# The second half of the last output block is stored through ScalarE's DMA queue

## The chip, the cores and the metric

One core of one Trainium2 chip runs the kernel. Its engines are TensorE (PE, with its weight loads PEld), VectorE (DVE), ScalarE (ACT), GpSimd (POOL) and SyncE (SP); SP computes nothing and issues DMAs. The metric is the time of one execution on the device in microseconds (us), as the median of several runs. A profile shows one execution more closely: its span runs from the first to the last instruction of the program.

## What is computed

Sparse attention over 4 batches of 8 heads, 768 positions and 64 channels a head, followed by a gated linear layer. All tensors are fp32. The reference, cut down:

```python
scores = scale * np.matmul(q, k.transpose(0, 1, 3, 2)) - slopes * dist
scores = np.where(is_global | is_local, scores, -1e9)      # 8 global, 96 local keys
a = softmax(scores)
x = np.matmul(a, v)                                        # then (4, 768, 512)
gate = sigmoid(causal depthwise conv of x with 5 taps)
out = (gate * (x @ w_val)) @ w_out                         # (4, 768, 512)
```

## The kernel before

The sequence of each batch is cut into two halves of three blocks of 128 rows, so there are eight phases (`phases`, `ph` 0 to 7). For each phase the kernel computes the attention of four pairs of heads, the convolution, the gate, the value product (`val`, L930) and the output product (`outp`, L957), which leaves each block of 128 rows by 512 columns in PSUM. ACT or DVE copies it to SBUF (`evac_o`, L969) and SP stores it to HBM (`store`, L981). All instructions stand in one straight line; the order of all of them is written out in the table `ORDER`, and each engine executes its own in that order.

The last phase is treated apart. Its three blocks are named `LATE` and live in the tiles `late[0]` to `late[2]`. The last of them is cut into two halves of 256 columns (`parts` gives 2 for this block alone and 1 for every other), with `h` 0 and 1: two smaller groups of matmuls, two smaller copies on ACT and two smaller stores. So `h` is 1 for one store of the program.

The stores of the late blocks do not stand in the straight line. Before them stands a branch, `tc.If(slow[0])` at L1114: a flag, read from a tile on every engine, says whether inputs lie outside what the fast path covers. If it is set, the function `general` computes everything again. Otherwise all engines jump over `general`. After the branch SP issues the four late stores, in the order block 0, block 1, block 2 with h 0, block 2 with h 1 (`for key in behind_general: store(*key)`, L1118). A hint to load the code behind the branch early is given to SP, ACT and DVE (L1110).

On each engine the jump is followed by a short piece of code that brings the semaphores to the counts that the other path would have left: SP does this for the eight semaphores `DMAHW0` to `DMAHW7`, which the landings of DMAs raise in turn, and ACT for its own counter of finished instructions. At the very end (line L1345, where the program is closed) SP waits for the eight DMA semaphores by number, one instruction each, and then all five engines meet in a barrier. In the kernel before, no engine but SP issues a DMA.

Of the kernel before, what the change touches and what calls it, by code (L numbers as in the profile page):

```python
# [132 lines left out]
P = 128  # L133
# [144 lines left out]
def attention_moe(ctx, tc, qT, kT, kg, vw, v, counts_in, wt, wb, out):  # L278
    nc = tc.nc
# [81 lines left out]
    T = {}  # L361
# [17 lines left out]
    def width(s):  # L379
        return P if block(*steps[s]) == 0 else WIN  # L380
# [42 lines left out]
    for ph in range(NPH):  # L423
        todo = [(g, k) for g in range(ph * NP, ph * NP + NP) for k in range(blocks(g))]
        n = BATCH[phases[ph][2]]
# [101 lines left out]
    def biases(e, h, part):  # L527

        cols = slice(0, P) if part == 0 else slice(P, P + WIN)
        x = -8.0 * 2.0 ** -(h + 1)  # L530
        if e == ACT:
            nc.scalar.mul(bias[:, h, cols], dist[:, cols], x)
            return
        engine(e).tensor_scalar(
            out=bias[:, h, cols], in0=dist[:, cols], scalar1=x, scalar2=1.0, op0=ALU.mult, op1=ALU.mult,
        )

    for h in range(H):
        for part, cost in enumerate(({DVE: 0.13, POOL: 0.34, ACT: 0.24}, {DVE: 0.19, POOL: 0.42, ACT: 0.28})):
            plan.add(("BIAS", h, part), 3 * (h // 2) + part - 1 + 0.1 * (h % 2), cost,  # L540
                     lambda e, h=h, part=part: biases(e, h, part), [("DIST", part)])
# [180 lines left out]
    def chunks(q, k):  # L722
        n = pieces(step[2 * q, k])[0]
        return [(j, c) for j in range(2) for c in range(n)]
# [72 lines left out]
    for q in range(NPAIR):  # L797
        for k in range(blocks(2 * q)):
# [4 lines left out]
            n = len(chunks(q, k))  # L803
# [5 lines left out]
    for g, (ph, p) in enumerate(groups):  # L809
        for k in range(blocks(g)):  # L810
            s = step[g, k]
            n = width(s)
# [141 lines left out]
    def parts(ph, k):  # L954
        return 2 if (ph, k) == (NPH - 1, phases[ph][2] - 1) else 1
# [25 lines left out]
    def store(ph, k, h):  # L981
        b, k0, _ = phases[ph]
        r0, n = (k0 + k) * P, DM // parts(ph, k)
        if (ph, k) in LATE and not general_is_behind:
            behind_general.append((ph, k, h))
            return
        w = n // (2 if ph in IN_TWO else 1)
        for c in range(0, n, w):
            nc.sync.dma_start(out[b, r0 : r0 + P, h * n + c : h * n + c + w], T["ob", ph, k, h][:, c : c + w])

    sent = []

# [29 lines left out]
    def add_outputs(ph):  # L1022
# [6 lines left out]
        for k in range(nk):  # L1029
            for h in range(parts(ph, k)):  # L1030
                n = parts(ph, k)
                for c in range(NC):
                    key = ("OM", ph, k, h, c)
                    deps = [("GH", ph, c), ("GL", ph, c), ("WP", NC + c), ("WH", NC + c)]
                    if c:
                        bank = [("OM", ph, k, h, c - 1)]
                    elif (ph, k) == (NPH - 1, nk - 1):
                        bank = [("FC",)]
                    else:
                        bank = plan.ring("moe", 2, key, [("OE", ph, k, h)])  # L1040
                    deps += bank
                    if ph == 0 and c == 0:
                        deps += [("WP", NC + i) for i in range(NC)]
                    if (ph, k, h, c) == (NPH - 1, 0, 0, 0):
                        deps += [("FV",)]
                    plan.add(key, u + U_O + O_T * (4 * k + c) / 12 + 0.5 * h, {PE: 0.649 / n},
                             lambda e, ph=ph, k=k, h=h, c=c: outp(ph, k, h, c), deps)
                    if c == 0:
                        plan.opening(key, bank)
                key = ("OE", ph, k, h)  # L1050
                plan.add(key, u + U_O + U_OE * (k + 1), {ACT: 0.6 - 0.215 * h} if (ph, k) in LATE else {ACT: 0.6 - 0.215 * h, DVE: 0.605 - 0.25 * h},
                         lambda e, ph=ph, k=k, h=h: evac_o(e, ph, k, h),
                         [("OM", ph, k, h, NC - 1)] + ([] if (ph, k) in LATE else plan.ring("ob", 3, key, [("ST", ph, k, h)])))
                key = ("ST", ph, k, h)
                plan.add(key, u + U_O + U_OE * (k + 1), {SP: 0.5}, lambda e, ph=ph, k=k, h=h: store(ph, k, h),
                         [("OE", ph, k, h)] + ([("BR",)] if (ph, k) in LATE else []), P * DM * 4 // n)
                if (ph, k) not in LATE:
                    sent.append(key)
# [59 lines left out]
    for key in behind_general:  # L1118
        store(*key)
# [229 lines left out]
```

## Time and profile before

| | |
|---|---|
| median of 3 runs | 251.1 us (250.1 to 251.37) |
| the profiled execution | 249.76 us |
| its span | 248.0 us |
| PE, DVE, ACT, POOL busy | 96%, 86%, 72%, 53% of the span |
| q1, the DMA queue that SP feeds | 23040 packets, 45.21 MB |

The profiled execution lies 1.3 us under the median of the runs, and 1.76 us of it lie outside its span. An engine's name with a q, as ACTq or SPq, stands for its sequencer: waits on semaphores, branches, and the issue of DMAs. Such instructions are not counted as busy time. A DMA has a start (its issue), a duration (how long the sequencer took to issue it) and a time to landing (from the issue to the last of the 16 DMA engines reporting).

### The profile page before, as it was taken

The page shows a single profiled execution, that of the slowest core. Times are in us where ns is not written, and L with a number is a line of the kernel's source. Part 1 is how long each engine was busy: PE and PEld are TensorE (multiplying, and loading weights), DVE is VectorE, ACT ScalarE, POOL GpSimd, SP SyncE. Part 2 cuts the span into 40 slices and gives each one's busy share as a digit, 9 for nine tenths or more (in the row PEclk, how much of TensorE's full clock was granted, in tenths as well). Part 3 has the DMA queues.
Part 4 walks back from the last instruction along what each step waited for, and adds up shares of the span by engine and source line. Part 5 has one row for each costly group of instructions (what it writes and reads, how often), then busy time and mean ns, then how long its engine had stood idle before and what let it go on. Part 6 is the DMA issues. An engine that isn't in the chain of part 4 may idle for free.

```text
span 248.0 us, 10366 instructions
## 1 busy us (share of the span) xinstructions
PE 238.8 (96%) x4037; PEld 204.7 (83%) x4041; DVE 213.4 (86%) x822; ACT 179.6 (72%) x600; POOL 130.4 (53%) x264
## 2 busy tenths in 40 slices
PE   8998788999999999999999999999999999999993
PEld 3556577888899888988899788898899889988993
DVE  3997999998979989898989989898979979989620
ACT  3999899998998488877967589886678388422202
POOL 6989999999317530364064533455419741810220
PEclk9999999999999999999999999999999999999999
DMA  5999598161298054529558289791079507200303
GB/s 181 401 397 386 200 336 284 36 187 52 61 306 306 3 186 186 167 100 272 187 172 256 84 272 345 221 312 48 7 261 402 200 25 227 73 4 0 127 8 134
DMA packets 23095, 45.94 MB, mean 185 GB/s; under 512 B 2688, under 2 KB 13696, under 8 KB 23040
## 3 DMA queue, kind: packets, MB, share of 16 engines
q1 hardware_dynamic: 23040, 45.21, 53.4%
q8 instruction: 34, 0.56, 0.9%
q14 instruction: 21, 0.17, 0.2%
HBM read 38.91 MB, written 6.29 MB: 182 GB/s over the span
## 4 chain that ended last, share of the span: by engine, by line
PE 80%; DVE 12%; POOL 4%; DMA 1%; issue 1%; ACT 0%; SPq 0%; DVEq 0%; POOLq 0%
PE o L963 26%; PE val L935 25%; PE x L765 11%; PE s L685 9%; PE pt L734 5%; PE pt L737 4%; DVE gate L881 3%; DVE t L693 3%; POOL p L720 3%; DVE wh L562 2%; DMA counts_i<-in_counts 1%; DVE xl L872 1%; DVE wy L557 1%; POOL wvh L328 1%; DVE wy L565 1%
## 5 line engine op out<-in xcount | busy, mean ns | idle before, releaser
L720 POOL TENSOR_SCALAR p<-p,rs 128x168 f32<-128x168 f32 (+1 forms) x152 | 66.3, 450 | 55.1 <-DVE rs L714 36.4
L704 ACT ACTIVATE p<-t,mins 128x168 f32<-128x168 f32 (+1 forms) x192 | 81.5, 430 | 13.8 <-DVE mins L693 12.2
L881 DVE SCALAR_TENSOR_TENSOR gate<-x,cwt,gate 128x384 f32<-128x384 f32 x128 | 76.2, 614 | 1.1
L693 DVE CUSTOM_DVE_ANT_0 t<-s,bias 128x168 f32<-128x168 f32 (+1 forms) x192 | 54.1, 318 | 7.6 <-PE s L685 7.5
L935 PE MATMUL val<-xh,wvh 128*128 128x384 f32 x128 | 44.4, 347 | 0.2 <-DVE gate L944 0.2
L326 ACT COPY a<-pt 128x384 f32<-128x384 f32 (+2 forms) x79 | 35.3, 473 | 11.7 <-PE pt L734 7.6
L935 PE MATMUL val<-xl,wvh 128*128 128x384 f32 x128 | 41.8, 327 | 0.0
L935 PE MATMUL val<-xh,wvl 128*128 128x384 f32 x128 | 41.7, 326 | 0.0
L963 PE MATMUL o<-woh,gh 128*128 128x512 f32 (+1 forms) x100 | 39.1, 391 | 0.0
L704 ACT ACTIVATION_READ_ACCUMULATOR p<-t,mins 128x1 f32 x192 | 37.6, 196 | 0.0
L963 PE MATMUL o<-woh,gl 128*128 128x512 f32 (+1 forms) x100 | 37.2, 372 | 0.0
L963 PE MATMUL o<-wol,gh 128*128 128x512 f32 (+1 forms) x100 | 37.1, 371 | 0.0
L765 PEld LDWEIGHTS x<-a,v 56*64 56x64 f32 (+1 forms) x2112 | 33.7, 135 | 4.0 <-issue 1.1
L685 PE MATMUL s<-rk,rq 64*64 64x168 f32 (+1 forms) x768 | 35.8, 304 | 1.1 <-issue 0.9
L765 PE MATMUL x<-a,v 56*64 56x64 f32 (+1 forms) x2112 | 35.8, 219 | 0.8 <-DVE x L863 0.7
L685 PEld LDWEIGHTS s<-rk,rq 64*64 64x64 f32 x768 | 25.8, 132 | 8.9 <-issue 6.0
L952 POOL TENSOR_TENSOR gl<-gate,gh 128x384 fp32r<-128x384 f32 x24 | 24.1, 1008 | 11.8 <-ACT gh L326 5.0
L935 PEld LDWEIGHTS val<-xh,wvh 128*128 128x128 f32 x128 | 24.2, 189 | 1.8 <-DVE gate L944 0.5
L935 PEld LDWEIGHTS val<-xl,wvh 128*128 128x128 f32 x128 | 24.2, 189 | 0.5 <-DVE xl L872 0.2
L935 PEld LDWEIGHTS val<-xh,wvl 128*128 128x128 f32 x128 | 24.2, 189 | 0.0
L944 DVE SCALAR_TENSOR_TENSOR gate<-gate,val 128x384 f32<-128x384 f32 x32 | 17.4, 549 | 4.7 <-PE val L935 4.5
L963 PEld LDWEIGHTS o<-wol,gh 128*128 128x128 f32 x100 | 18.9, 189 | 2.4
(101 smaller groups left out, 351.0 us busy)
## 6 DMA issues: line engine op xcount, KB each, us to landing
v<-in_vw SPq DMA_DIRECT2D x40, 384.0 KB, 5.6
rq<-in_qT SPq DMA_DIRECT2D x32, 192.0 KB, 5.3
rk<-in_kT SPq DMA_DIRECT2D x16, 252.0 KB, 4.8
out<-ob SPq DMA_DIRECT2D x15, 256.0 KB, 4.8
w<-in_wb SPq DMA_DIRECT2D x7, 512.0 KB, 5.8
again<-in_wb SPq DMA_DIRECT2D x7, 512.0 KB, 5.9
rk<-in_kT SPq DMA_DIRECT2D x16, 200.0 KB, 4.9
out<-ob SPq DMA_DIRECT2D x12, 128.0 KB, 1.8
```

What stands on the lines that cost most here:

```text
L326: nc.scalar.copy(dst, src)
L685: nc.tensor.matmul(T["s", step[g, k], j][half], T["rq", g][r, k * P + i * HQ : k * P + (i + 1) * HQ], T["rk", g][r, c0 : c0 + n], start=Tr ...
L693: nc.vector.tensor_tensor_reduce(out=t[:, :n], in0=T["s", s, j], in1=bias[:, h, :P] if n == P else bias[:, h, P:], op0=ALU.add, op1=ALU.mi ...
L704: nc.scalar.activation(p_of(s, j), T["t", s, j][:, :n].rearrange("p (c w) -> p c w", c=pieces(s)[0]), AF.Exp, bias=mins[:, s, j : j + 1], ...
L720: engine(e).tensor_scalar(out=pr, in0=pr, scalar1=rs, scalar2=1.0, op0=ALU.mult, op1=ALU.mult)
L734: nc.tensor.transpose(pt[n // 4][:, n % 4 * P : n % 4 * P + P], src, ident)
L765: nc.tensor.matmul(T["x", 2 * q + r][j * D : (j + 1) * D, c0 : c0 + HQ], v[rows, slot], a[rows, i, n * j + c], start=c == 0, stop=c == use ...
L881: nc.vector.scalar_tensor_tensor(out=gt, in0=src, scalar=w, in1=gt, op0=ALU.mult, op1=ALU.add)
L935: nc.tensor.matmul(T["val", ph, m], (wvh, wvh, wvl)[r][:, c, m * P : (m + 1) * P], woven((T["xh", g], T["xl", g], T["xh", g])[r][:, : size ...
L944: nc.vector.scalar_tensor_tensor(out=t, in0=t, scalar=1.0, in1=T["val", ph, m].rearrange("p (b a) -> p a b", a=2), op0=ALU.add, op1=ALU.mult)
L952: engine(e).tensor_sub(tile_of(("gl", ph, m), [P, HT], F32R, "gl", G_B)[:, :n], T["g", ph, m], T["gh", ph, m][:, :n])
L963: nc.tensor.matmul(T["o", ph, k, h], (T["gh", ph, c], T["gl", ph, c], T["gh", ph, c])[r][:, cols], woven((woh, woh, wol)[r][:, c])[:, h * ...
```

## The change

The function `store` takes its queue by `h`: SP's where `h` is 0, ACT's where it is 1. Only the last half block has `h` 1. The line numbers behind this place grow by one.

```diff
         for c in range(0, n, w):
-            nc.sync.dma_start(out[b, r0 : r0 + P, h * n + c : h * n + c + w], T["ob", ph, k, h][:, c : c + w])
+            queue = nc.scalar if h else nc.sync
+            queue.dma_start(out[b, r0 : r0 + P, h * n + c : h * n + c + w], T["ob", ph, k, h][:, c : c + w])
```

On SP, behind the branch, the stores of the late blocks stand so in the kernel before (`late_86` to `late_88` are the three late tiles; in brackets the semaphores waited for):

```order
L1114 UNCONDITIONAL_BRANCH [waits DMAHW0_49,DMAHW1_49,DMAHW2_49,DMAHW3_49,DMAHW4_49,DMAHW5_49,DMAHW6_49,DMAHW7_49]
L989 DMA out<-late_86 128x512 [waits DMAHW1_49,DMAHW4_49,DMAHW0_49,DMAHW7_49,DVE_49,Activation_49]
L989 DMA out<-late_87 128x512 [waits DMAHW5_49,DVE_49,Activation_49]
L989 DMA out<-late_88 128x256 [waits DMAHW6_49,DVE_49,Activation_49]
L989 DMA out<-late_88 128x256 [waits Activation_49]
L1345 UNCONDITIONAL_BRANCH
```

And so in the changed kernel:

```order
L1115 UNCONDITIONAL_BRANCH [waits DMAHW0_49,DMAHW1_49,DMAHW2_49,DMAHW3_49,DMAHW4_49,DMAHW5_49,DMAHW6_49,DMAHW7_49]
L990 DMA out<-late_86 128x512 [waits DMAHW1_49,DMAHW5_49,DMAHW0_49,DMAHW7_49,DVE_49,Activation_49]
L990 DMA out<-late_87 128x512 [waits DMAHW6_49,DVE_49,Activation_49]
L990 DMA out<-late_88 128x256 [waits DVE_49,Activation_49]
L1346 UNCONDITIONAL_BRANCH
```

One store has left SP, and the three that stay have moved up by one semaphore each: they report to `DMAHW5`, `DMAHW6` and `DMAHW7`, where the four reported to `DMAHW4` to `DMAHW7`.

On ACT, the last rows of the program in the kernel before (`g_gate` is a tile of `general`, which the jump passes over):

```order
L1250 ACTIVATE g_gate<-g_gate 128x3072
L1232 REGISTER_ALU
L1232 COMPARE_AND_BRANCH
L1232 UNCONDITIONAL_BRANCH
L1114 UNCONDITIONAL_BRANCH
L1345 UNCONDITIONAL_BRANCH
```

And in the changed kernel:

```order
L1251 ACTIVATE g_gate<-g_gate 128x3072
L1233 REGISTER_ALU
L1233 COMPARE_AND_BRANCH
L1233 UNCONDITIONAL_BRANCH
L1115 UNCONDITIONAL_BRANCH
L990 DMA out<-late_88 128x256
L1346 UNCONDITIONAL_BRANCH
```

The store now stands on ACT between the jump over `general` and the program's end. It waits there for `DMAHW1`, `DMAHW4`, DVE's counter and ACT's own, in three instructions (two that only wait, and the issue itself), and reports to `DMAHW4`. The instructions of all engines ahead of the branch are the same in both kernels.

## Rows read from the trace of the kernel before

**Rows 1.** The page's first part: busy us, share of the span, instructions.

```profile
PE 238.8 (96%) x4037; PEld 204.7 (83%) x4041; DVE 213.4 (86%) x822; ACT 179.6 (72%) x600; POOL 130.4 (53%) x264
```

**Rows 2.** The chain that ended last, from 237 us: start us, us, what.

```profile
237.15 6.55 PE o L963 x39
243.70 0.02 issue
243.73 0.72 ACT late L975 x2
```

**Rows 3.** Timeline of ACT from 244.2 us: start us, us, engine, line, operation.

```profile
244.06 0.38 ACT L975 ACTIVATE late<-o 128x256 f32<-128x256 f32 x1
```

**Rows 4.** Timeline of SP, from 241 us, and of the last store alone.

```profile
241.72 3.42 SPq L989 DMA_DIRECT2D out<-late  x4
...
244.71 0.42 SPq L989 DMA_DIRECT2D out<-late  x1
```

**Rows 5.** Line 989, third late store, then the fourth: issue ns, start; landing us.

```profile
L989 SPq DMA_DIRECT2D out<-late x1: 524/524/524, 244.1 to 244.1; - x1
...
DMA to landing us min/median/max: 2.6/2.6/2.6
...
L989 SPq DMA_DIRECT2D out<-late x1: 422/422/422, 244.7 to 244.7; - x1
...
DMA to landing us min/median/max: 2.4/2.4/2.4
```

**Rows 6.** Line 1345, the program's end: duration ns min/median/max, first and last start.

```profile
L1345 SPq EVENT_SEMAPHORE  x4: 28/28/28, 245.2 to 245.4; - x4
...
L1345 SPq EVENT_SEMAPHORE  x4: 28/28/28, 245.8 to 247.1; - x4
L1345 SPq DRAIN  x2: 7/7/7, 247.2 to 247.2; - x2
L1345 PEldq DRAIN  x1: 8/8/8, 246.0 to 246.0; - x1
...
L1345 ACTq DRAIN  x1: 8/8/8, 244.6 to 244.6; - x1
...
L1345 ACTq BRANCH_PREFETCH_HINT  x1: 45/45/45, 0.7 to 0.7; - x1
```

**Rows 7.** Waits of SP's queue from 245.3 us: total us, times, longest us.

```profile
SPq L1345 <- DMA out<-late: 1.5, 4, 0.6
```

**Rows 8.** Line 1114, the branch, on the engines' sequencers.

```profile
L1114 SPq EVENT_SEMAPHORE  x8: 17/17/17, 235.0 to 238.2; - x8
L1114 SPq COMPARE_BRANCH  x1: 70/70/70, 234.5 to 234.5; - x1
...
L1114 POOLq COMPARE_BRANCH  x1: 45/45/45, 238.3 to 238.3; - x1
...
L1114 POOLq EVENT_SEMAPHORE  x1: 17/17/17, 240.8 to 240.8; - x1
L1114 PEldq COMPARE_BRANCH  x1: 4114/4114/4114, 241.6 to 241.6; - x1
L1114 ACTq COMPARE_BRANCH  x1: 68/68/68, 244.1 to 244.1; - x1
L1114 ACTq EVENT_SEMAPHORE  x1: 17/17/17, 244.5 to 244.5; - x1
```

**Rows 9.** Issues of SP's own DMAs elsewhere: the program's first, and the longest.

```profile
L368 SPq DMA_DIRECT2D counts_i<-in_counts x1: 383/383/383, 0.8 to 0.8; - x1
...
L582 SPq DMA_DIRECT2D again<-in_wb x7: 327/422/1628, 144.4 to 190.5; - x7
```

**Rows 10.** The page's sixth part: KB each, median us from issue to landing.

```profile
out<-ob SPq DMA_DIRECT2D x12, 128.0 KB, 1.8
...
out<-late SPq DMA_DIRECT2D x2, 256.0 KB, 3.5
out<-late SPq DMA_DIRECT2D x2, 128.0 KB, 2.5
```

**Rows 11.** DMA engines from 244.69 to 247.2 us: 40 slices, busy tenths; then queues.

```profile
DMA  9972100979997624889996210300910000000000
...
q8 instruction: 1, 0.02, 3.5%
```

## The prediction

> **What bounds the kernel now.** I read the busy times first: PE is busy for 96% of the span, no other engine for more than 86% [rows 1]. Then the chain that ended last: from 237.15 us it is the output product on PE, up to 243.70, and then two copies on ACT, up to 244.45 [rows 2]. The reader is to see that the store cannot touch PE's part: it comes behind the last matmul, and the instructions ahead of the branch are the same. What the change can move lies between the last copy and the end of the span, 248.0 - 244.45 = 3.5 us, so I took these 3.5 us apart.
>
> The last copy runs from 244.06 for 0.38 us, to 244.44 [rows 3]. SP issues the last store at 244.71 and is done with it at 245.13 [rows 4]; it was held for 0.27 us, most of it because the third store was being issued, from 244.1 for 524 ns [rows 5]. The fourth store lands 2.4 us after its start, at 247.1; the third 2.6 us after 244.1, at 246.7 [rows 5]. From 245.2 SP goes through its closing waits. The first four pass within 0.2 us, so one that finds its semaphore ready costs 0.2 / 3 = 0.07 us [rows 6]. The other four stand from 245.8 to 247.1 [rows 6], and all four are ended by landings of late stores, 1.5 us of waiting together [rows 7]. The last is passed at 247.1, SP's drains follow at 247.2 [rows 6], and the barrier takes the rest to 248.0. So the span ends 0.9 us after the last landing, whichever queue that store came from. ACT (244.6) and PE (246.0) are at the barrier earlier [rows 6] and have slack of 2.6 and 1.2 us.
>
> **Why the last landing is late.** Late stores of 128 KB take 2.5 us to land, twelve others of that size took 1.8 [rows 10]. The DMA engines' activity shows why: from slice 16 to 21 (245.7 to 246.1 us, slices of 0.063 us) most engines work, on the fourth store; behind that stands a thin trickle (a tenth or so) to slice 30, about 246.6 us, and nothing after it [rows 11]. One or two engines of the 16 are behind the others, and the store has landed only when the last has reported. A load of code runs in the same stretch [rows 11], and PE's sequencer waited 4.1 us at the branch from 241.6 [rows 8]. That these loads are what put an engine behind is my reading, not shown. What matters is that an engine with a backlog ends at the same time if the last store comes 0.1 us earlier.
>
> **The change part by part.**
>
> *Only one store moves.* `h` is 1 for one store of the program; the order lists show one DMA fewer on SP and one more on ACT. The bytes, the tile and the wait for ACT's copy stay.
>
> *SP loses an issue of 422 ns* [rows 5]. It ends its third at 244.66 and goes to its closing waits 0.47 us earlier. This is worth nothing: they end by the landings.
>
> *ACT gains two waits and an issue.* ACT passes its semaphore update at 244.5 and reached its final drain at 244.6 [rows 8, 6]. Between these now stand the two waits, 0.07 us each by SP's row; they find the DMA semaphores ready since 238.2 [rows 8], and the wait for ACT's copy is met. The issue starts at 244.6 + 0.14 = 244.7 to 244.8, against 244.71: 0 to 0.1 us later. What ACT saves by not standing behind SP's third store it spends on its own path. Behind the store on ACT stands the final drain alone; ACT comes to the barrier at about 245.2 instead of 244.6, still 2 us early.
>
> *The price of an issue on ACT* has no row. SP's issues take 327 ns at the least, 422 in the middle and 1628 at the most [rows 9]. ACT's sequencer does other things as fast as SP's: the branch in 68 ns against 70, a semaphore in 17 against 17 [rows 8]. I take 327 to 422 ns, nearest to SP's short and middle ones: the issue ends between 245.0 and 245.2, against 245.13, which is -0.1 to +0.1 us for the landing on an engine without a backlog, and 0 on the one that is behind. The first DMA of a queue need not cost more: SP's first took 383 ns [rows 9]. I take 0 for the landing: 247.1 as before.
>
> *The order of the closing waits.* The moved store now reports to `DMAHW4`, the three others to `DMAHW5` to 7, and SP waits by number. Before, the semaphore that came last was also the last in line. Now, if the moved store lands last, SP passes `DMAHW4` at 247.1 and still has three ready waits to go through: 3 x 0.07 = +0.2 us. If the third store lands last, it stands last in line and this costs nothing. The fourth lands 0.4 us after the third now, and I take the first case.
>
> *Sum:* issue and landing -0.1 to +0.1, middle 0; waits 0 to +0.2, taken at +0.15. The span goes from 248.0 to about 248.15 and the profiled execution from 249.76 to 249.9. That execution lies 1.3 us under the median of the runs; put on the median, 251.1 + 0.15 gives 251.2 us, 0.06% slower. The runs of before spread over 1.3 us (250.1 to 251.37), so a measurement of this kernel tells about 0.5%, or 1.25 us, from no change.
>
> **The rivals.**
>
> *The third store lands last.* On the engine that is behind, packets of the fourth store, coming by a second queue, could be served in turn with those of the third instead of after them. The total work of that engine is the same, so the last landing stays near 247.1, but it is now that of `DMAHW7`, the last in line, and the three waits are hidden: +0, 251.1 us. Against it stands that the fourth lands 0.4 us after the third and that no row shows two queues at once.
>
> The Trainium skill, "DMA: Bandwidth & Descriptors", section "Queues, rings and completion order", states that each DMA engine goes round its queues packet by packet, and that SP and ACT each own a queue; by that rule this rival would be the outcome, and no row of this trace can show it.
>
> *A real gain.* If the fourth store were issued right at 244.44 and landed without delay, SP would still wait for the third, at 246.7. The most that can be won is 247.1 - 246.7 = 0.4 us: 250.7 us. For it speaks the 0.27 us that SP held the store; against it ACT's own 0.3 us and the engine with the backlog.
>
> *Slower: the code behind ACT's jump is not there.* In this kernel ACT jumped in 68 ns, but PE's jump held it for 4.1 us, and POOL, past its branch at 238.3, reached its semaphore update only at 240.8, 2.5 us later [rows 8]. If ACT's longer code behind the branch falls into a part that has to be loaded, the store would start 2.4 to 4.0 us later and with it the end: 253.5 to 255.1 us. That decides from a delay of 1.25 us on. Against it: the hint that ACT gets at 0.7 us is the same [rows 6], and only a few instructions are added. An issue as long as SP's longest, 1628 ns, would go the same way, more mildly: 1.2 us above the median one, 0.2 for the waits, 252.5 us.
>
> **How the numbers follow.** The forecast gets 0.62, the third store landing last 0.18, the gain 0.08, code that has to be loaded 0.05, a long issue 0.04, and 0.03 are left for something else. The first three lie between 250.7 and 251.3. The range adds what the runs spread on either side, and reaches towards the long issue: 249.9 to 252.4 us. Faster by over 0.5% no mechanism here can do, since 0.4 us is 0.16%; 0.03 stand for scatter. Slower by over 0.5% takes code that is loaded, a long issue, or scatter: 0.08. Within 0.5%: 0.89.
>
> **What would show it.** One DMA on ACT's queue, starting at 244.7 to 244.8 relative to a last copy that ends at 244.44 (0.3 us behind it), of 330 to 420 ns; a landing about 2.4 us later; SP's closing waits with one long wait on `DMAHW4` and three quick ones behind it, or one at the end; a span of 248.0 to 248.3. I am wrong if ACT's branch or its issue takes over 1 us, if the landing from ACT's queue takes over 3 us, or if anything ahead of 243.7 us has moved by more than the runs' scatter.

## The result and the profile after

| | before | after |
|---|---|---|
| median | 250.24 us (9 runs, 249.55 to 251.37) | 251.67 us (9 runs, 251.26 to 252.17) |
| the profiled execution, its span | 249.76 us, 248.0 us | 251.45 us, 249.6 us |
| ratio after to before | | 1.0052 (95% interval 1.0033 to 1.0071) |

The changed kernel is slower by half a percent, with the interval on both sides of the 0.5% that the prediction set as a bound: 1.4 us between the medians, 1.6 us between the spans. The forecast was 251.2 us in 249.9 to 252.4, 0.15 us above before. The time lies in that range, but the difference is nearly ten times the forecast one, and the mechanism that made it was among the rivals, with a chance of 0.04.

Ahead of the last copy nothing moved. The chain that ended last (start us, us, what) has in the kernel after:

```profile
237.17 6.55 PE o L963 x39
243.73 0.02 issue
243.75 0.72 ACT late L975 x2
```

Those are [rows 2] with starts 0.02 to 0.03 us later. The difference is behind them, on ACT. The timeline of ACT in after, behind its last copy (start us, us):

```profile
244.78 2.21 ACTq L990 DMA_DIRECT2D out<-late  x1
```

And line 990 in after from 244.6 us (ns min/median/max, first and last start; then the time to landing):

```profile
L990 ACTq EVENT_SEMAPHORE  x2: 17/28/38, 244.6 to 244.7; - x2
L990 ACTq DMA_DIRECT2D out<-late x1: 2209/2209/2209, 244.8 to 244.8; - x1
...
DMA to landing us min/median/max: 3.8/3.8/3.8
```

ACT begins to issue the store at 244.78, and the issue takes 2209 ns where SP took 422 [rows 5]. The landing is 3.8 us after the start, at 248.5. The rows around it, of the branch (line 1115) and of the program's end (line 1346), in after:

```profile
L1115 ACTq COMPARE_BRANCH  x1: 68/68/68, 244.1 to 244.1; - x1
L1115 ACTq EVENT_SEMAPHORE  x1: 17/17/17, 244.6 to 244.6; - x1
...
L1346 SPq EVENT_SEMAPHORE  x4: 27/28/28, 244.6 to 244.8; - x4
...
L1346 SPq EVENT_SEMAPHORE  x4: 28/28/28, 248.6 to 248.7; - x4
L1346 SPq DRAIN  x2: 7/7/7, 248.8 to 248.9; - x2
...
L1346 ACTq DRAIN  x1: 148/148/148, 247.0 to 247.0; - x1
```

The jump itself takes 68 ns, as in [rows 8]; ACT reaches its final drain at 247.0, where it stood at 244.6 [rows 6]. SP's closing waits have become one long wait (total us, times, longest us), and three ready ones in the 0.2 us behind it:

```profile
SPq L1346 <- DMA out<-late: 3.7, 1, 3.7
```

The DMA engines from 244.6 to 249 us in 40 slices of 0.11 us, busy tenths, then the queues (packets, MB, share):

```profile
DMA  9961599610011106000000000049981000000000
...
q1 hardware_dynamic: 225, 0.26, 16.9%
q10 hardware_dynamic: 144, 0.13, 9.0%
q8 instruction: 1, 0.02, 1.5%
q14 instruction: 1, 0.01, 1.0%
```

The store's bytes do not move until slice 26, at 247.5, 0.5 us behind the end of the issue; in slices 16 to 25, 246.4 to 247.4, no packet starts. So the transfer was not slowed by anything on the DMA engines: it was not there yet. The store's own queue is q10, which the kernel before doesn't have.

From 241 to 249 us the two queues that load instructions, q8 and q14, moved two packets each in both kernels. One of each falls into the time of the long issue. The one on q14 has 8 KB and starts 1.1 us behind ACT's branch. From 245.15 to 245.2 us the queue's line is:

```profile
q14 instruction: 1, 0.01, 88.6%
```

It takes 0.7 us (88.6% of 16 engines for 0.05 us), to 245.9, and the issue ends 1.1 us after that. The one on q8 has 16 KB and starts at 246.3, 0.8 us behind the end of PE's jump. The kernel before has the same two, at 245.1 and 246.5, and no DMA on ACT that could have waited for them. Whether the issue waits for one of them is taken up behind the experiments.

The sum by terms, from start and end of these rows:

| from the last copy to the end | before | after | difference, us |
|---|---|---|---|
| start of the issue | 244.71 | 244.78 | +0.07 |
| the issue | 0.42 | 2.21 | +1.79 |
| from its end to the landing | 245.13 to 247.1 | 246.99 to 248.5 | -0.4 |
| from the landing to the last drain | 247.1 to 247.2 | 248.5 to 248.8 | +0.2 |
| the barrier to the end of the span | 247.2 to 248.0 | 248.8 to 249.6 | 0 |

The sum is +1.6 to +1.7 us, against +1.6 us between the spans.

### The profile page after: what moved, and what is told of

Same layout as the page of the kernel before. It is cut to its first block, busy times and chain, and to the rows that moved or that the text cites. A ratio compares the mean times of both kernels' runs of the same rounds, so it can differ in the third digit from the quotient of the medians.

```text
span 249.6 us, 10368 instructions
## 1 busy us (share of the span) xinstructions
PE 238.4 (96%) x4037; PEld 204.6 (82%) x4041; DVE 213.6 (86%) x822; ACT 179.7 (72%) x600; POOL 130.3 (52%) x264
## 4 chain that ended last, share of the span: by engine, by line
PE 82%; DVE 8%; POOL 4%; ACT 2%; issue 1%; DMA 1%; SPq 0%; DVEq 0%; POOLq 0%
PE o L963 26%; PE val L935 24%; PE x L765 11%; PE s L685 10%; PE pt L734 5%; PE pt L737 4%; POOL p L720 2%; DVE t L693 2%; DVE gate L881 2%; DMA counts_i<-in_counts 1%; DVE wh L562 1%; ACT p L704 1%; ACT a L326 1%; POOL wol L602 0%; POOL wvh L328 0%
```

## The experiments

The question is why an issue on ACT costs 2.2 us. The theories are named in the expectations; each kernel is the changed one with the edit shown, unless said otherwise.

### An earlier store on ACT

```diff
-            queue = nc.scalar if h else nc.sync
+            queue = nc.scalar if h or (ph, k) == (NPH - 2, 1) else nc.sync
```

> The changed kernel, and besides both half-width stores of block 1 of the phase before the last go through ACT's queue too. They stand on ACT behind the read of the flag at 231.3 us, where ACT is idle until 241. Four theories of the 2209 ns that ACT's only issue took. T1, the first issue on ACT's queue costs that much and later ones do not: 2.2 us for the first at 231.4, 0.33 to 0.45 us for the second and for the last store at 244.8; last landing 247.1, 0.2 us of closing waits, span 248.0 to 248.4, level with the kernel before within 0.3%. T2, every issue on ACT costs 2.2 us: three of 2.2 us, span 249.6, 0.5% slower than before. T3, ACT's issue is held until SP's late stores have landed: last issue 2.2 us as in the changed kernel, span 249.6. T4, it is the place just behind the jump: 0.3 to 0.45 us for the two early ones, 2.2 us for the last, span 249.6.

Two more stores, of a block of the phase before, go to ACT. Line 990 in this run, from 231 us and from 244.6 us:

```profile
L990 ACTq DMA_DIRECT2D out<-ob x2: 385/416/448, 231.4 to 231.8; - x2
...
L990 ACTq DMA_DIRECT2D out<-late x1: 342/342/342, 244.8 to 244.8; - x1
...
DMA to landing us min/median/max: 2.4/2.4/2.4
```

Neither the first issue (385 ns) nor the last (342 ns) is long, which none of the four theories had as a whole: it isn't that every issue on ACT is long, nor every first one, nor the place at the program's end alone. The span is 248.3 us, and the ratio to before 1.0018 (1.0001 to 1.0035): with a cheap issue the moved store costs 0.3 us in the span. Line 1346 from 246 us shows most of it: four closing waits behind the landing at 247.2, one for it and three that are ready:

```profile
L1346 SPq EVENT_SEMAPHORE  x4: 28/28/28, 247.2 to 247.4; - x4
```

### An earlier load on ACT, at the start

```diff
+    spare = const.tile([P, 2, 2], I32, name="spare")
+    nc.scalar.dma_start(spare, counts_in ... .to_broadcast([P, 2, 2]))
```

> The changed kernel with one more DMA: ACT's first instruction loads 2 KB (the counts again, into a tile that nobody reads) at 0.8 us; ACT's table load comes behind it, and ACT has no work before 5.15 us. T1, once per execution: 2.2 us for the load, which lies in ACT's idle time, and 0.33 to 0.45 us for the last store, 243 us later; span 248.0 to 248.4, level with before within 0.3%. T1b, what the first issue brings in is lost again in 240 us of other work on ACT, or is per tensor: 2.2 us for both, span 249.6, 0.5% slower. T2, T3 and T4 also give 2.2 us for the last store and 249.6; T2 gives 2.2 for the load, T3 and T4 give 0.4 for it.

The load's issue in ACT's timeline, where it is the first row:

```profile
0.82 0.39 ACTq L373 DMA_DIRECT2D spare<-in_counts  x1
```

And the last store's, at line 993 in this run:

```profile
L993 ACTq DMA_DIRECT2D out<-late x1: 363/363/363, 247.9 to 247.9; - x1
```

A load of another tensor 247 us earlier is enough to make the last issue cheap (363 ns). The ratio is 1.011 all the same, since the run lost 3 us at its start, where I had thought the small load free.

> The kernel before, all stores on SP, with the same additional 2 KB load on ACT's queue at 0.8 us: what the early load costs by itself. T1: the issue takes 2.2 us, the table load behind it ends at about 4.3 us instead of 2.1, ahead of ACT's first work at 5.15; span 248.0, level with before within 0.3%. T3 and T4: the issue takes about 0.4 us; span 248.0 as well.

The kernel before with that same load has a ratio of 1.0133 (1.011 to 1.0156) and a span of 251.3 us: the 3 us are the price of the load alone. The page's DMA issues in the run with the store on ACT (KB, us to landing):

```profile
spare<-in_counts ACTq DMA_DIRECT2D x1, 2.0 KB, 5.5
counts_i<-in_counts SPq DMA_DIRECT2D x1, 2.0 KB, 5.7
```

In the kernel before, SP's load of the counts takes 2.8 us and ACT's first computation starts at 5.15 us; here it starts at 7.95. The two loads each read the same 16 bytes 128 times. That they hold each other up for this reason is my reading: no run loaded other bytes.

### All four late stores on ACT

```diff
-            queue = nc.scalar if h else nc.sync
+            queue = nc.scalar if (ph, k) in LATE else nc.sync
```

> All four late stores go through ACT's queue, so SP issues nothing behind 234.5 us and no store of SP is in flight when ACT issues at 244.8. T1 and T4: 2.2 us for the first, 0.33 to 0.55 us for each of the other three, issues end at 248.4, last landing 2 us later at 250.4, span about 251.3 us (1.3% slower than before). T2: four of 2.2 us, issues end at 253.6, span 256.5. T3: no wait for SP, all four 0.33 to 0.55 us, issues end at 246.6, span 249.4.

One run, 253.22 us. Line 990, all four issues, and the one from 245 to 246 us alone:

```profile
L990 ACTq DMA_DIRECT2D out<-late x4: 362/422/2105, 245.3 to 248.4; - x4
...
L990 ACTq DMA_DIRECT2D out<-late x1: 2105/2105/2105, 245.3 to 245.3; - x1
```

The first takes 2105 ns, the others 362 to 460. SP issued no late store here, so the long issue doesn't come from SP's stores being in flight. It is the first one behind the jump, and only that.

### A first store on ACT in the middle

```diff
-            queue = nc.scalar if h else nc.sync
+            queue = nc.scalar if h or (ph, k) == (3, 1) else nc.sync
```

> The changed kernel, and besides the store of block 1 of phase 3 goes through ACT's queue, somewhere between 110 and 145 us, amid ACT's exponentials. After e1 and e2, where ACT's first issue took 385 to 394 ns at 0.8 us and at 231 us, and the later last store 340 to 363, while e3 again gave 2105 ns for a first issue at 245.3 us, these theories stand. U1, ACT's first issue costs 2.2 us unless something close before it (the program's start, the read of the flag at 230.8 us) has just done the same: 2.2 us here, 0.35 for the last store. U2, it costs 2.2 us only where it is the first and stands behind the jump: 0.4 us here, 0.35 for the last. Either way the last landing is near 247.1 and the span 248.2 (U2), or up to 2 us more where ACT's stall of 2.2 us holds up the attention (U1).

ACT's very first DMA stands at 153.86 us, and then the last store:

```profile
L990 ACTq DMA_DIRECT2D out<-ob x1: 382/382/382, 153.9 to 153.9; - x1
...
L990 ACTq DMA_DIRECT2D out<-late x1: 343/343/343, 245.0 to 245.0; - x1
```

A first issue in straight code costs 382 ns, and U1 falls. The ratio, 1.0025 (1.0013 to 1.0037), is that of the first experiment again.

### Without the jump, store on ACT and on SP

Both kernels leave out the branch, the hint and `general`; the late stores then stand in the straight line. One has the last store on ACT, the other on SP:

```diff
-            if len(run) - n == HINT_AHEAD:
-                tc.mark_branch_hint_location("slow path", ...)
...
-    with tc.If(slow[0], label="slow path"):
-        general(...)
```

> The changed kernel without the branch and without the general path (it leaves out the second computation for inputs outside the fast path's cover; the flag is still computed and read by SP, no longer by ACT). The last store is ACT's only DMA, at about 244.5 us, in straight code. U1: 2.2 us, last landing 248.3, 1.8 us later than in the same kernel with the store on SP. U2, the jump is a condition: 0.35 us, last landing level with the store on SP to 0.2 us.

> The kernel before without the branch and without the general path (left out as in the one with the store on ACT), all stores on SP: the mate to compare it with. No engine jumps, so PE does not stand 4.1 us behind one and no code is loaded for it at 243.3 us. If the loads of code put a DMA engine behind, as I read the profile, the four late stores land with no straggler: the last one 1.7 to 1.9 us after its issue instead of 2.4, span 247.2 to 247.5. If not, 2.4 us and 248.0.

ACT's only DMA of the program, in the timeline of the first:

```profile
243.56 0.72 ACT L975 ACTIVATE late<-o 128x256 f32<-128x256 f32 x2 [0.40 <-PE o L963]
244.31 0.37 ACTq L990 DMA_DIRECT2D out<-late  x1
```

Both late half stores of the second, line 989 from 244.4 us, with their time to landing:

```profile
L989 SPq DMA_DIRECT2D out<-late x2: 332/368/405, 244.4 to 244.8; - x2
...
DMA to landing us min/median/max: 1.7/1.8/1.8
```

And the only queue of the second that loads instructions from 241 to 249 us (packets, MB, share):

```profile
q14 instruction: 1, 0.01, 0.3%
```

Without the jump the first and only issue on ACT takes 372 ns and starts 0.03 us behind the copy, which ends at 244.28. So the jump is a condition of the long issue, as U2 has it. Against the kernel before, the ratios are 0.9981 (0.9971 to 0.999) on ACT and 0.9996 (0.9981 to 1.0011) on SP. Against each other the two kernels differ by more than their scatter: medians of 249.56 and 250.02 us in ten runs each, means 0.37 us apart (95% interval 0.15 to 0.59). But not all of that is the move. ACT's last copies in the second kernel:

```profile
243.97 0.72 ACT L975 ACTIVATE late<-o 128x256 f32<-128x256 f32 x2 [0.41 <-PE o L963]
```

They end at 244.69 against 244.28, so of the 0.5 us between the two spans (247.2 and 247.8) 0.4 us lie ahead of the moved store. Behind the last copy it is 3.0 us on ACT and 3.1 on SP: in this pair of executions the move by itself, with nothing in its way, is worth 0.1 us. Where the 0.4 us come from is not shown.

The second kernel also bears on the landings. One packet is left on the queues that load instructions, where the kernel before had four in that stretch, and its half stores land in 1.7 to 1.8 us instead of 2.4 to 2.6 [rows 5]. The span is 247.8 all the same, above the 247.2 to 247.5 that I had expected: the last copy ends 0.24 us later than in the kernel before.

### Is it the landing's code load, or PE's jump?

Edit to the kernel before: PE is added to the engines that get the hint.

```diff
-... engines=(SP, Activation, DVE))
+... engines=(SP, Activation, DVE, PE))
```

> The kernel before with one edit: PE too gets the hint to load the code behind the branch early. If the load of code for PE's jump at 241.6 us puts a DMA engine behind, the jump takes about 0.1 us instead of 4.1 and the last store lands 0.4 to 0.6 us earlier: span 247.4 to 247.6, 0.2% faster. If the straggler has another cause: last landing 247.1 and span 248.0 as before.

The ratio is 1.0037 (1.0022 to 1.0053): no gain, and I had expected one. Line 1114, PE's jump:

```profile
L1114 PEldq COMPARE_BRANCH  x1: 388/388/388, 241.8 to 241.8; - x1
```

The queues that load instructions from 242 to 246 us (packets, MB, share):

```profile
q8 instruction: 1, 0.02, 2.2%
q14 instruction: 1, 0.01, 1.2%
```

And the time to landing of the two half stores, line 989 from 244.4 us:

```profile
DMA to landing us min/median/max: 2.6/2.6/2.7
```

PE's jump falls from 4114 ns [rows 8] to 388. Of the two 16 KB loads on q8 that the kernel before has here, at 243.3 and at 246.5 us, the first still comes, at 242.9, and the second, the one in [rows 11], does not. The 8 KB load on q14 comes too, at 245.4. The half stores still take 2.6 us. So the late landing goes neither with the jump's wait nor with the load in [rows 11]. It may go with the two loads that are left; no run took away these alone.

### No hint for ACT, ACT's code shifted, a DMA in the skipped path

Three kernels, run once each, for other ways in which the jump could make the issue long.

```diff
# first
-... engines=(SP, Activation, DVE))
+... engines=(SP, DVE))
# second, ahead of the branch
+        for i in range(3):
+            nc.scalar.copy(idle_tile[:, i], ident)
# third, in general
-            nc.sync.dma_start(w, raw(i))
+            (nc.sync if i else nc.scalar).dma_start(w, raw(i))
```

> The changed kernel with the hint to load the code behind the branch early given to SP and DVE alone, no longer to ACT. So far ACT's issue takes 2.1 to 2.2 us only where it is ACT's first in the execution and stands behind the jump (the changed kernel, e3); 0.34 to 0.39 us in all other cases (e1, e2, e5, e6). V1, the 2.2 us have to do with the code that the hint brings in: the jump itself now takes 2.5 to 4 us and the issue 0.35. V2, they have not: the jump takes 2.5 to 4 us and the issue 2.2 on top, last landing near 251, span 252.

> The changed kernel with three more copies on ACT (the identity matrix into a tile that nobody reads), behind the read of the flag at 231 us, where ACT is idle: every later instruction of ACT stands three places further on in its code, and no DMA is added. If the 2.2 us come from where the store falls in the blocks in which code is loaded, they go: 0.35 us for the issue, span 248.2. If they come from its being ACT's first DMA behind a jump, 2.2 us as in the changed kernel, span 249.6.

> The changed kernel with one load inside the general path given to ACT's queue. That path is jumped over, so the load is never executed; it only stands ahead of the store in ACT's program. If something that was set when the program was put together goes with a queue's first DMA in program order, it now goes with the skipped one and the store takes 0.35 us, span 248.2. If the state is one of the run, the store is still the first to be executed: 2.2 us, span 249.6.

In the first, ACT's branch and the instruction behind it (line 1115), and then the issue in ACT's timeline:

```profile
L1115 ACTq COMPARE_BRANCH  x1: 50/50/50, 244.2 to 244.2; - x1
...
L1115 ACTq EVENT_SEMAPHORE  x1: 17/17/17, 247.0 to 247.0; - x1
```

```profile
247.21 2.01 ACTq L990 DMA_DIRECT2D out<-late  x1
```

The issue in the second, at line 992, and in the third:

```profile
L992 ACTq DMA_DIRECT2D out<-late x1: 2502/2502/2502, 245.0 to 245.0; - x1
```

```profile
L990 ACTq DMA_DIRECT2D out<-late x1: 2192/2192/2192, 245.0 to 245.0; - x1
```

Without its hint ACT is held behind the jump for 2.8 us, until 247.0, and the issue takes 2009 ns on top of that: 253.45 us. So the wait at the jump and the long issue come one after the other. The Trainium skill, "Runtime: NRT & Kernel Launch", section "Instruction fetch mechanics", states that a taken branch to code that isn't loaded waits for a load. That agrees with the first of the two, 2.8 us here; the second isn't told there. Each of the two has an 8 KB load of its own on q14 in this run: one from 245.2 us, while the jump holds ACT, and one that the changed kernel doesn't have, within the issue, from 247.5 to 247.7 us:

```profile
q14 instruction: 1, 0.01, 16.0%
```

So this run doesn't tell whether the issue waits for code as well. Three instructions more ahead of the branch leave the issue at 2502 ns: a shift by three places doesn't spare it, and larger ones were not tried. A DMA of ACT in the path that is jumped over leaves it at 2192 ns: to spare the wait a DMA must have been executed, not only stand in the program.

### Other work on ACT between the jump and the store

```diff
+    for i in range(8):
+        nc.scalar.copy(idle_tile[:, i % 3], late[2][:, 256:384])
```

> The changed kernel with work for ACT put between its jump over the general path and its store: eight copies of 128x128 into a tile that nothing reads, with a load of the function table ahead of them. One such table load took 1.28 us in the kernel after, and one such copy 0.29 us in the run with idle copies ahead of the branch (a pipelined one somewhat less): so ACT works about 1.28 + 8 x 0.25 = 3.3 us behind its jump, from 244.6 to about 247.9, before it comes to the store. The question is when the 2 us of the issue behind the jump are spent. W1: the jump sets something going that takes about 2 us by itself (2.2 us from 244.8 in the kernel after) and runs beside ACT's other work; by 247.9 it is over, the issue takes 0.34 to 0.46 us, the store lands some 2 us later at about 250.0 to 250.5, and the span is about 251.1 to 251.6. W2: the price is paid when the first DMA is executed behind the jump, however late: the issue takes 2.0 to 2.5 us, the store lands at about 251.7 and the span is about 252.8. Either way the kernel is slower than after by the copies (3.3 us under W2, 1.5 us or so under W1); what tells is the duration of the issue.

One run, 252.34 us. ACT behind its jump, which takes 68 ns at 244.83:

```profile
245.43 1.28 ACT L1121 ACT_TABLE_LOAD   x1 [0.23 <-ACTq L1116]
246.72 1.29 ACT L1121 COPY idle_tile<-late 128x128 f32<-128x128 f32 x6
247.91 0.38 ACTq L991 DMA_DIRECT2D out<-late  x1
```

With 2.5 us of other work ahead of it the issue takes 381 ns. W1 fits: the 2 us run out beside ACT's other work. So do the other runs: from the first instruction behind the jump to the end of the long issue it is 2.4 us in the kernel after (244.6 to 247.0) and 2.2 us in the run without ACT's hint (247.0 to 249.2); here the issue starts 2.6 us behind that instruction, which stands at 245.3. From the end of the last copy to the end of the span it is 5.3 us (245.2 to 250.5), still 0.2 more than in the kernel after (244.5 to 249.6), since the other work is in the way.

**What the runs settle.** Of twelve kernels and the changed one, those in which an issue on ACT took 2.0 to 2.5 us are the five in which it was ACT's first executed DMA and stood right behind its taken jump, with nothing but waits between (after, all four on ACT, no hint, shifted, DMA in the skipped path). It took 0.34 to 0.46 us wherever one of the two was missing. Four of the five have one run each, and so has the one with other work between.

What the jump leaves unready stays open, but the traces have a candidate that these experiments did not test: the 8 KB load on q14. It starts 1.1 to 1.6 us behind ACT's branch in every run that has the branch, and in neither of the two without it. Each long issue ends a like time behind the end of such a load, and so does the wait at ACT's jump that the hint otherwise takes away (start and end of the packet in the trace, us):

| run, and what ends | the load | ends at | behind the load |
|---|---|---|---|
| after, issue | 245.18 to 245.89 | 246.99 | 1.10 |
| all four on ACT, first issue | 245.63 to 246.18 | 247.42 | 1.25 |
| no hint, wait at the jump | 245.25 to 245.77 | 246.99 | 1.23 |
| no hint, issue | 247.59 to 248.10 | 249.22 | 1.11 |
| shifted, issue | 245.86 to 246.17 | 247.48 | 1.30 |
| DMA in skipped path, issue | 245.34 to 246.06 | 247.15 | 1.09 |

Where an earlier DMA made the issue short, the same load comes, but the issue is over 0.05 to 0.2 us before it starts; so the store's own instruction was there. In the last run the issue starts 1.3 us behind its end. That the long issue waits for this load isn't shown: both may follow the jump each by itself, and no run kept the jump without the load. Why a DMA executed 247 us earlier spares the wait isn't in the traces. Nor is it told apart whether time alone makes the issue cheap in the last run, or the table load and copies that filled it.

## Why the prediction was wrong where it was

**The price of an issue on ACT** is the term that failed: taken at 327 to 422 ns, measured at 2209. It was bounded by SP's rows, and the short ones were chosen because ACT's sequencer is as fast as SP's elsewhere and SP's first DMA was short. Both reasons are true as far as they go: ACT's first DMA in straight code took 372 to 394 ns in the runs. But every row used was of an issue in straight code or behind earlier issues. None was of a first issue behind a jump, and the upper bound of 1628 was too low as well. The bound that would have held stood in [rows 8]: what POOL and PE did behind the same jump took 2.5 to 4.1 us. The prediction used those rows only for code that has to be loaded.

**The long issue** was named as a rival, at 252.5 us and 1.4 us above the median of the runs; measured were 1.4 us. Its size was right and its chance, 0.04, was not. (With the 0.05 for code that has to be loaded the two mechanisms alone had 0.09, and "slower by over 0.5%" was given 0.08.) The prediction's last paragraph gave an issue of over 1 us and a landing of over 3 us as the signs of being wrong: both came, 2.2 and 3.8 us.

**The start of the issue** held: 244.7 to 244.8 was forecast, 244.78 came, 0.3 us behind the last copy. What ACT saves by not standing behind SP's third store it spends on its jump, its counter and two waits. Without the jump it starts 0.03 us behind the copy.

**The closing waits** held: three ready ones behind `DMAHW4`, +0.2 us, here and in the first experiment.

**The landing.** An engine with a backlog was to make it 247.1 whatever the issue. In after, the issue ended so late that the backlog was over: 1.5 us from the end of the issue to the landing, against 2.0, which gave back 0.4 us. That code loads make the backlog was my reading, with the load in [rows 11] as the sign. That load can't be the one: it starts at 246.5, when most engines have worked the last store off [rows 11], and with PE's hint it is gone and the half stores still take 2.6 us. The kernel on SP without the jump, whose only load in this stretch starts at 248.0, behind all landings, lands them in 1.8 us. That fits the two loads that PE's hint leaves (16 KB at 242.9, 8 KB at 245.4), but no run took away a load alone.

**The rivals.** The third store doesn't land last: in the first experiment, with both queues at work, SP's long closing wait is for the moved store, and the three behind it are ready. The Trainium skill, "DMA: Bandwidth & Descriptors", section "Queues, rings and completion order", has each DMA engine go round its queues packet by packet. Here two queues at work together did not change which store ended last. A gain of up to 0.4 us: with the jump in place none came (1.0018 and 1.0025); without it the profiled pair has 0.1 us behind the last copy. The code behind ACT's jump was there: 68 ns for the jump. What came instead had a like size, 2.2 us against 2.4 to 4.0, but at the issue; whether that too is a wait for code is open.

**The level.** 251.2 us was 0.15 us on top of a median of three runs, 251.1; nine runs put it at 250.24. Had the base been right, the forecast would have been 250.4, and the measured 251.67 is 1.3 us above that. The time came into the range partly by this.

## What to carry to other kernels

Before a DMA is moved to an engine that has issued none, ask where its first one would stand: in straight code it cost 0.38 us here, close behind a taken jump 2.0 to 2.5 us. If it must stand there, let the engine execute a useful DMA earlier, and not a second load of what another queue is reading: at the program's start that cost 3 us here. The Trainium skill, "DMA: Bandwidth & Descriptors", section "Issuing engines are not separate DMA queues", puts the gain of a second issuer at the sequencer's time only. Here that time was 0.27 us of holding, and it was spent on the new engine's own waits and on the order of the closing ones.

## What was not expected of the hardware

- The first DMA that ACT executes, behind a taken jump: 2009 to 2502 ns of issue in five runs, 381 ns in the one run with 2.5 us of other work between.
- Two loads that broadcast the same 16 bytes to 128 partitions at once: 5.5 and 5.7 us to landing, against 2.8 us for one alone.
- A hint took PE's jump from 4114 to 388 ns and one of two 16 KB loads of code away, and the half stores still landed after 2.6 us, against 1.8 without the jump.
